# A PSUM bank reserved for the sums, another first transpose, and rounding steps tied to the gated rows, in a hash-attention and SwiGLU kernel

## The chip, the core and the metric

The kernel runs on one core of one Trainium2 chip. The metric is the device time of one execution in microseconds, median of three runs. An execution begins with its inputs in DRAM and ends when the output is in DRAM. The core has a matrix engine (PE, with its weight loads shown apart as PEld), a vector engine (DVE), a scalar engine (ACT), a general engine (POOL) and an engine that only issues transfers (SP). Each engine works through its own list of instructions; engines wait for each other through semaphores.

## The reference

Attention with a hash mask, and a gated feed-forward block on its result, all in 32-bit floats:

```python
# q, k, v: (4, 8, 768, 64); proj: (64, 6)
q_bits = einsum('bhsd,dk->bhsk', q, proj) > 0          # six sign bits for each row
k_bits = einsum('bhsd,dk->bhsk', k, proj) > 0
mask   = q_bucket[:, :, :, None] == k_bucket[:, :, None, :]
scores = where(mask, q @ k^T / 8, -1e9)
attn   = exp(scores - max);  attn = attn / (sum(attn) + 1e-9)
x      = attn @ v                                      # as (3072, 512) for what follows
g, val = x @ w_gate, x @ w_val                         # w: (512, 1536), 64-bit floats
out    = (g * sigmoid(g) * val) @ w_out                # w_out: (1536, 512)
```

The three weight matrices come in as 64-bit floats. The kernel reads them as pairs of 32-bit words and rounds them to 32-bit floats itself.

## The kernel before

**Rounds.** Work is cut into 32 rounds. A round is one batch, one pair of heads and one half of the 768 queries (`u` in the main loop L711 to L769 counts in steps of `NCH` = 6 key chunks; round number = `u / 6`). In each round TensorE computes six scores (`score`, L456: for both heads a 32-bit product of the transposed query and key, then a bf16 product of their sign bits, which pushes pairs of different buckets down), ACT takes the exponential of each score tile (L467) into a ring of six weight tiles, TensorE multiplies them by v (`attend`, L476), DVE adds the six weight tiles up (`add`, L487 and L491), TensorE sums that over the partitions with a matrix of ones (`norm`, L501, tile `sum`), and DVE takes its reciprocal (L504) and scales the product with v (L506, L507). Only then is the half of `xT` done that the feed-forward block reads.

**Front of a pair of heads.** `front` (L380) makes the transposed q and k and their sign bits. For the first pairs it transposes on TensorE (`tps`, L388; ACT copies out, L391) and hashes with `hash_bits` (`hps`, L405; ACT takes signs, L398; DVE scales those of k, L400). From the sixth pair on DVE transposes (L431), and `hash_blocks` (L411 to L415) does all four hash products into one PSUM tile.

**PSUM.** There are eight banks. `av` has one. All others are one pool of seven, `banks` (L66): the two score tiles of each chunk, `tps`, `hps`, `sum`, the six accumulators of an up-projection (`up`) and the three of a down-projection (`po`). A tile waits until the last reader of the tile that had its bank before is done.

**Feed-forward.** From round 8 (`LATE`, L450) each round also runs a list of `atoms`: single products of Strassen schemes. `both` (L554) is one up-projection of 14 atoms of size 1: seven products for the gate and seven for the value, in turn, with ACT copies (L591), DVE sums (L537), tanh on ACT (L519) and two DVE steps (L520, L524). Its last two products, in the two `a` accumulators, are read by L520 and L524 at the end of the list. `down_strassen` (L612) has seven atoms of size 2 per chunk. Weights of the up-projection come back from a DRAM scratch `ram` by POOL's transfers (`bring`, L322) into two `places`.

**Rounding the weights.** `prepare` (L345) is a generator of single DVE steps. For each of 36 pieces of 128 x 512 weights, `narrow` (L294) has three: L303, L305 and L308. Before them ACT makes two passes over the piece (`scale_to`, L286 and L287), which need the piece's 512 KB of words. `load_words` (L251) has POOL fetch the words, a few pieces ahead, into the buffers that a finished piece leaves. After eight pieces of a block, `form` (L324) adds four sums per pair (L337) and writes them to `ram`. The main loop advances this generator by hand: `prepare_on(2)` and `prepare_on(6)` in each round ahead of `norm` (L737, L739), and in the atom loop 0.7 steps for each unit of size (L759 to L761). `scale_ahead` (L290) puts the ACT passes of the next two or three pieces into ACT's list; it is called before `attend` and after every atom. The first piece also carries a test of how the words round: L282, L283, L285, L300 and L310 (through `bits_a` and `bits_b`).

**Order.** `manual_schedule` is on: instructions stand in each engine's list in the order of the program text, and none is moved. So the place of a call in the main loop decides what an engine does first. In the gating rounds `chores` puts the steps of the next pair's front behind single atoms: for the hash products after the second atom.

Of the kernel before, what the change touches and what calls it, by code (L numbers as in the profile page):

```python
# [8 lines left out]
FP32 = mybir.dt.float32  # L9
BF16 = mybir.dt.bfloat16  # L10
I32 = mybir.dt.int32
U16 = mybir.dt.uint16
ALU = mybir.AluOpType
# [5 lines left out]
def kernel(  # L19
# [11 lines left out]
    nc = tc.nc  # L31
# [3 lines left out]
    P = 128  # L35
# [27 lines left out]
    wraw = ctx.enter_context(tc.tile_pool(name="wraw", bufs=2))  # L63
    dram = ctx.enter_context(tc.tile_pool(name="dram", bufs=1, space=bass.MemoryType.DRAM))
    av_ps = ctx.enter_context(tc.tile_pool(name="av_ps", bufs=1, space=PSUM))
    banks = ctx.enter_context(tc.tile_pool(name="ps", bufs=7, space=PSUM))  # L66

    ctx.enter_context(tc.manual_schedule())

    def bank(name):  # L70
        return banks.tile([P, 512], FP32, tag="ps", name=name)


    pairs = [(b, pr) for b in range(B) for pr in range(NP)]
# [176 lines left out]
    def load_words(done, queue=nc.gpsimd):  # L251
        for i in range(len(words), len(pieces)):
# [6 lines left out]
            else:  # L259
# [2 lines left out]

    progress = {"late": False, "piece": 0, "scaled": 0, "blocks": 0}

    bits_a, bits_b = (formed[x].rearrange("p n m -> p (n m)").bitcast(I32)[:, 0:PIECE]
                      for x in range(2))

    def scale_to(count):

        free = NJ * (progress["blocks"] + 2)
        if free >= 2 * NJ * DF // PIECE:
            free = len(pieces)
        for i in range(progress["scaled"], min(count, free, len(pieces))):
            t, w = words[i], pieces[i][0]
            top = t.rearrange("p f w -> p (f w)").bitcast(U16)
            top = top.rearrange("p (f w) -> p f w", w=4)[:, :, 1]
            if i == 0:


                nc.vector.tensor_single_scalar(bits_a, t[:, :, 0], 29, op=ALU.logical_shift_right)  # L282
                nc.vector.tensor_scalar(bits_b, t[:, :, 0], scalar1=28, scalar2=1,  # L283
                                        op0=ALU.logical_shift_right, op1=ALU.bitwise_and)
                nc.vector.tensor_tensor(bits_a, bits_a, bits_b, op=ALU.add)  # L285
            nc.scalar.activation(w, t[:, :, 1].bitcast(FP32), AF.Copy, scale=2.0**-112)  # L286
            nc.scalar.activation(t[:, :, 0], top, AF.Copy, scale=2.0**-13 * (1 + 2.0**-17))  # L287
            progress["scaled"] = i + 1
# [5 lines left out]
    def narrow(i):  # L294
        progress["piece"] = i
        t, w = words[i], pieces[i][0]
        lo, hi = t[:, :, 0], t[:, :, 1]
        wi = w.bitcast(I32)
        if i == 0:
            nc.vector.tensor_tensor(bits_b.bitcast(FP32), bits_a, lo, op=ALU.not_equal)  # L300
        scale_to(i + 1)

        nc.vector.tensor_single_scalar(wi, wi, 3, op=ALU.logical_shift_left)  # L303
        yield True
        nc.vector.scalar_tensor_tensor(out=wi, in0=hi, scalar=-(1 << 31), in1=wi,  # L305
                                       op0=ALU.bitwise_and, op1=ALU.bitwise_or)
        yield True
        nc.vector.tensor_tensor(wi, wi, lo, op=ALU.add)  # L308
        if i == 0:
            nc.vector.scalar_tensor_tensor(out=w, in0=bits_b.bitcast(FP32), scalar=1e4, in1=w,  # L310
                                           op0=ALU.mult, op1=ALU.add)
        progress["piece"] = i + 1
        load_words(i)
        yield True
# [50 lines left out]
    def prepare_on(n):  # L365
        for _ in range(n):
            next(preparing, None)
# [12 lines left out]
    def front(n):  # L380
# [27 lines left out]

        def hash_blocks():

            tile_ = bank("hps")  # L411
            for i, (name, half) in enumerate((name, half) for name in "kq" for half in range(2)):
                nc.tensor.matmul(tile_[i * BLOCK : (i + 1) * BLOCK, 0:HQ],  # L413
                                 hash_w[:, 0:BLOCK], T[name, n][:, half * HQ : (half + 1) * HQ],
                                 start=True, stop=True)  # L415

            def evict(name, half):
                i = 2 * (name == "q") + half
                ps = tile_[i * BLOCK : (i + 1) * BLOCK, 0:HQ]
                for to in (0, D):  # L420
                    scale = sign(name, half, slice(to, to + BLOCK), ps)
                    if scale:
                        more.append(scale)

            more = []
            return [lambda at=at: evict(*at) for at in
                    (("k", 0), ("k", 1), ("q", 0), ("q", 1))] + [lambda: [f() for f in more] and None]
# [9 lines left out]
        turns = [lambda x=x: transpose(*x) for x in order]  # L437
        hashes = [lambda x=x: hash_bits(*x) for x in order]
        if n == 0:
            return [turns[2], turns[0], turns[1], hashes[2], hashes[0], hashes[1], turns[3],  # L440
                    hashes[3]]
        return turns + hashes

# [49 lines left out]
    def norm(u):  # L493
        n, half, _ = units[u]
        b, pr = pairs[n]
        if half == 0:
            xT[b, pr] = xp.tile([P, S], FP32, tag="xT", name="xT")
        ps = bank("sum")
        t = acc.pop((n, half))
        for h in range(2):  # L500
            nc.tensor.matmul(ps[h * D : (h + 1) * D, 0:HQ], ones, t[:, h, :], start=True, stop=True)  # L501
        a = av.pop((n, half))
        r = att.tile([P, HQ], FP32, tag="r", name="r", bufs=1)
        nc.vector.reciprocal(r, ps[:, 0:HQ])  # L504
        e = att.tile([P, 1], FP32, tag="e", name="e")
        nc.vector.tensor_scalar(e, a[:, HQ : HQ + 1], scalar1=EPS, scalar2=None, op0=ALU.mult)  # L506
        nc.vector.scalar_tensor_tensor(out=xT[b, pr][:, half * HQ : (half + 1) * HQ],  # L507
                                       in0=a[:, 0:HQ], scalar=e, in1=r,
                                       op0=ALU.add, op1=ALU.mult)
        if pr == NP - 1 and half == 1:  # L510
            push_ffn(b)
# [187 lines left out]
    def prepare_pair(count):  # L699
        for _ in range(count):  # L700
            rest.extend(f for f in steps.pop(0)() or [] if f)
# [2 lines left out]
        while todo:  # L704
            todo.pop(0)()

    prepare_pair(5)
    finish(rest)
    N = len(units)
    credit = ahead = 0.0  # L710
    for u in range(0, N, NCH):  # L711
        n, half, _ = units[u]
        gating = u >= LATE
# [3 lines left out]
                nc.gpsimd.memset(t[:, :, HQ:AW], 1.0)  # L717
        for c in range(NCH):
            score(u + c)
            if u == 0 and c in (1, 2, 4):  # L720
                prepare_pair(1)
                finish(rest)
            if c:
                add(u + c)
# [21 lines left out]
        if n + 1 < len(pairs):  # L746
            if half == 0:
                steps = front(n + 1)
                chores = [None, steps.pop(0), None, steps.pop(0)]
            else:  # L750
                chores = [None, steps.pop(0)]

        credit += 14 if n < 2 * NP else 15.75
        end = True
        while atoms and (credit > 0 or not end):
            size, atom, end = atoms.pop(0)
            credit -= size
            atom()
            ahead += 0.7 * size  # L759
            prepare_on(int(ahead))  # L760
            ahead %= 1  # L761
            scale_ahead()
            for _ in range(size):
                if chores:
                    step = chores.pop(0)
                    chores.extend(step and step() or [])
# [37 lines left out]
```

The softmax here doesn't subtract the row's maximum and nothing guards it: scores larger than these inputs give would overflow.

## Time and profile before

Median 1028.34 us (1027.86 to 1030.48); the profiled execution spans 1028.6 us.

| stage | us | what PE does |
|---|---|---|
| start | 0 to 8 | nine idle products, transposes and hashes of the first pair |
| rounds 0 to 7 | 8 to 113 | attention alone, weights are rounded beside it |
| rounds 8 to 13 | 113 to 306 | attention and up-projections of batch 0, weights are rounded beside it |
| rounds 14 to 31 | 306 to 863 | attention and feed-forward |
| end | 863 to 1029 | six up-projections and the last down-projections |

A period, in what follows, is the time from the first `up` of a round to the first product of the next round's feed-forward. Where nothing holds PE up, the profile shows two lengths: 27.99 us (438.24 to 466.23) for a round without hash products, and 28.97 us (409.27 to 438.24) for one with them. A time with two figures such as "204.88 0.81" in a line of the trace is start and duration in microseconds; "[2.47 <-ACT room L467]" is the idle time before it and what ended it. In the lines the tile `room` is an area shared by weights, ring tiles and weight pieces, and `wo`, `hid` and `words` hold pieces too.

### The profile page before, as it was taken

How to read it: one execution, taken by the hardware profiler on the slowest of the kernel's cores; microseconds unless marked ns; L12 is line 12 of the kernel's file. 1: busy time of each engine (PE TensorE's matmuls, PEld its weight loads, DVE VectorE, ACT ScalarE, POOL GpSimd, SP SyncE). 2: the span in 40 equal slices, each digit the busy share in tenths (PEclk: the TensorE clock that was granted, in tenths of full speed). 3: DMA queues.
4: the chain of work that ended last, by engine and by line, in shares of the span. 5: the costliest groups of instructions: out<-in, count | busy, mean ns of one | idle time of the engine just before them, and what ended most of it. 6: DMA issues, size and time to landing. Idle time of an engine off the chain costs nothing.

```text
span 1028.6 us, 12425 instructions
## 1 busy us (share of the span) xinstructions
PE 1014.7 (99%) x4597; PEld 610.6 (59%) x4597; DVE 624.5 (61%) x1012; ACT 418.8 (41%) x905; POOL 99.3 (10%) x192
## 2 busy tenths in 40 slices
PE   9999999999999999999999999999999999999998
PEld 4444455555557775555556677555555787555687
DVE  5999987869895445565656472565656451525521
ACT  6776647365452413544352421534435201232200
POOL 2212022321100000000000000000000000101000
PEclk9999999999999999999999999999999999999999
DMA  7656485744622114242321203233222000333101
GB/s 212 196 163 201 120 216 203 212 162 156 172 72 52 37 31 107 72 103 82 84 81 37 62 21 93 59 82 95 72 72 72 21 21 31 109 97 113 31 26 36
DMA packets 113884, 99.90 MB, mean 97 GB/s; under 512 B 86976, under 2 KB 97216, under 8 KB 113824
## 3 DMA queue, kind: packets, MB, share of 16 engines
q0 software_dynamic: 19104, 73.28, 21.7%
q1 hardware_dynamic: 93920, 25.64, 11.3%
q8 instruction: 36, 0.59, 0.2%
q10 hardware_dynamic: 800, 0.20, 0.1%
q14 instruction: 24, 0.20, 0.1%
HBM read 81.79 MB, written 17.30 MB: 96 GB/s over the span
## 4 chain that ended last, share of the span: by engine, by line
PE 81%; DVE 10%; issue 4%; DMA 3%; ACT 2%; POOL 1%; DVEq 0%; POOLq 0%
PE up L533 36%; PE po L533 21%; PE sc L464 11%; PE av L476 9%; DVE acc L491 2%; DMA words<-in_moe_w_out_dram 2%; DVE r L504 2%; PE sum L501 1%; DVE room L305 1%; PE hps L413 1%; DVE room L337 1%; DVE room L308 1%; ACT A L467 1%; PE hps L405 1%; DVE room L303 1%
## 5 line engine op out<-in xcount | busy, mean ns | idle before, releaser
L533 PE MATMUL up<-xT,room 128*128 128x384 f32 x768 | 263.5, 489 | 0.0
L533 PEld LDWEIGHTS up<-xT,room 128*128 128x128 f32 x768 | 143.9, 190 | 109.7 <-issue 15.2
L533 PE MATMUL up<-xc,room 128*128 128x384 f32 x576 | 198.3, 487 | 2.0 <-ACT hid L591 1.5
L464 PE MATMUL sc<-qT,kT 64*128 64x384 f32 x768 | 164.3, 498 | 7.3 <-DVE e L506 3.3
L533 PEld LDWEIGHTS up<-xc,room 128*128 128x128 f32 x576 | 109.0, 190 | 79.8 <-ACT hid L591 2.8
L537 DVE TENSOR_TENSOR c<-c,up 128x384 f32<-128x384 f32 x72 | 39.8, 552 | 151.9 <-PE up L533 151.9
L491 DVE TENSOR_TENSOR acc<-acc,A 128x768 f32<-128x768 f32 x128 | 122.7, 958 | 14.6 <-ACT A L467 1.6
L322 POOL DMA_DIRECT2D room<-ram x96 | 52.0, 542 | 671.9 <-PE up L533 662.4
L467 ACT ACTIVATE A<-sc 128x384 f32<-128x384 f32 x256 | 105.9, 492 | 7.9 <-PE sc L464 7.8
L464 PEld LDWEIGHTS sc<-qT,kT 64*128 64x128 f32 x768 | 69.6, 188 | 62.9 <-issue 45.5
L661 ACT COPY o<-po 128x256 f32<-128x256 f32 x48 | 17.9, 372 | 199.2 <-PE po L533 199.1
L504 DVE RECIPROCAL r<-sum 128x384 f32<-128x384 f32 x32 | 81.7, 2554 | 27.1 <-PE sum L501 27.1
L476 PE MATMUL av<-A,vraw 128*64 128x386 f32 x512 | 88.4, 487 | 0.0
L519 ACT ACTIVATE th<-c 128x384 f32<-128x384 f32 x72 | 37.6, 522 | 104.4 <-DVE c L537 104.2
L537 DVE TENSOR_TENSOR o<-o,po 128x256 f32<-128x256 f32 x36 | 15.2, 421 | 102.2 <-PE po L533 61.1
L467 ACT ACTIVATE room<-sc 128x384 f32<-128x384 f32 x128 | 54.3, 488 | 38.6 <-PE sc L464 38.3
L533 PE MATMUL po<-wo,hid 128*128 128x256 f32 x288 | 66.9, 382 | 0.0
L464 PE MATMUL sc<-qb,kb 64*128 64x384 bf16 x384 | 66.7, 324 | 0.2 <-DVE kb L400 0.2
L533 PE MATMUL po<-wo,room 128*128 128x256 f32 x288 | 66.3, 380 | 0.0
L533 PE MATMUL po<-room,hid 128*128 128x256 f32 x288 | 66.1, 379 | 0.0
L476 PEld LDWEIGHTS av<-A,vraw 128*64 128x64 f32 x512 | 36.8, 137 | 46.2 <-issue 45.3
L591 ACT COPY c<-up 128x384 f32<-128x384 f32 x72 | 34.4, 478 | 70.9 <-PE up L533 70.7
(113 smaller groups left out, 1041.3 us busy)
## 6 DMA issues: line engine op xcount, KB each, us to landing
room<-ram POOLq DMA_DIRECT2D x48, 512.0 KB, 4.7
room<-ram POOLq DMA_DIRECT2D x48, 384.0 KB, 3.9
vraw<-in_v_dram SPq DMA_DIRECT2D x16, 384.0 KB, 3.2
ram<-room POOLq DMA_DIRECT2D x12, 512.0 KB, 4.1
out_dram<-o SPq DMA_DIRECT2D x48, 128.0 KB, 1.7
qraw<-in_q_dram SPq DMA_DIRECT2D x48, 96.0 KB, 3.2
kraw<-in_k_dram SPq DMA_DIRECT2D x46, 96.0 KB, 3.4
words<-in_moe_w_out_dram POOLq DMA_DIRECT2D x8, 512.0 KB, 4.7
```

The costliest lines, as they stand in the source:

```text
L303: nc.vector.tensor_single_scalar(wi, wi, 3, op=ALU.logical_shift_left)
L322: nc.gpsimd.dma_start(places[k % 2][:, PARTS[go], :], ram[k % NG][:, PARTS[go], :])
L464: nc.tensor.matmul(sc[h], x["k", n][rows, ks], x["q", n][rows, qs], start=start, stop=not start)
L467: nc.scalar.activation(weights(u)[:, h, 0:HQ], sc[h], AF.Exp, scale=SCALE)
L476: nc.tensor.matmul(ps[h * D : (h + 1) * D, 0:AW], raws["v", n][:, h, c, :], a[:, h, :], start=c == 0, stop=c == NCH - 1)
L491: nc.vector.tensor_tensor(acc[n, half], acc[n, half], a[:, :, 0:HQ], op=ALU.add)
L504: nc.vector.reciprocal(r, ps[:, 0:HQ])
L519: nc.scalar.activation(th, g, AF.Tanh, scale=0.5)
L533: nc.tensor.matmul(ps, a, x, start=start and i == 0, stop=i == len(pairs_) - 1, skip_group_check=True)
L537: nc.vector.tensor_tensor(o, a, b, op=op)
L591: nc.scalar.copy(tile_of(g, spot), c)
L661: nc.scalar.copy(o, c)
```

## The change

Four edits. A pool of one bank, `sm_ps`, holds `sum` and the hash tile of `hash_blocks`; the shared pool shrinks from seven banks to six. The first pair's front transposes k before q, and does the second half of k after the first score and not before it; hash products in gating rounds move from the second atom to the fifth. The test on the first weight piece goes. In the atom loop, rounding steps go one per unit of size for the first ten units of a round's list (and then none), and ACT's passes are put ahead only from the sixth unit on. The aim is that sums no longer hold up the banks that scores need, and that the end of a round's gated rows is free of rounding work.

```diff
-    banks = ctx.enter_context(tc.tile_pool(name="ps", bufs=7, space=PSUM))
+    sm_ps = ctx.enter_context(tc.tile_pool(name="sm_ps", bufs=1, space=PSUM))
+    banks = ctx.enter_context(tc.tile_pool(name="ps", bufs=6, space=PSUM))
...
+    def odd_bank(name):
+        return sm_ps.tile([P, 512], FP32, tag="sm", name=name)
...
-    bits_a, bits_b = (formed[x].rearrange("p n m -> p (n m)").bitcast(I32)[:, 0:PIECE]
-                      for x in range(2))
...
-            if i == 0:
-                nc.vector.tensor_single_scalar(bits_a, t[:, :, 0], 29, op=ALU.logical_shift_right)
-                nc.vector.tensor_scalar(bits_b, t[:, :, 0], scalar1=28, scalar2=1,
-                                        op0=ALU.logical_shift_right, op1=ALU.bitwise_and)
-                nc.vector.tensor_tensor(bits_a, bits_a, bits_b, op=ALU.add)
...
-        if i == 0:
-            nc.vector.tensor_tensor(bits_b.bitcast(FP32), bits_a, lo, op=ALU.not_equal)
...
-        if i == 0:
-            nc.vector.scalar_tensor_tensor(out=w, in0=bits_b.bitcast(FP32), scalar=1e4, in1=w,
-                                           op0=ALU.mult, op1=ALU.add)
...
         def hash_blocks():
-            tile_ = bank("hps")
+            tile_ = odd_bank("hps")
...
         if n == 0:
-            return [turns[2], turns[0], turns[1], hashes[2], hashes[0], hashes[1], turns[3],
+            return [turns[0], turns[2], hashes[0], hashes[2], turns[1], hashes[1], turns[3],
                     hashes[3]]
...
-        ps = bank("sum")
+        ps = odd_bank("sum")
...
-    prepare_pair(5)
+    prepare_pair(4)
...
-            if u == 0 and c in (1, 2, 4):
+            if u == 0 and c in (0, 1, 2, 4):
                 prepare_pair(1)
...
-                chores = [None, steps.pop(0)]
+                chores = [None, None, None, None, steps.pop(0)]
...
+        part = 0
         while atoms and (credit > 0 or not end):
             size, atom, end = atoms.pop(0)
             credit -= size
             atom()
-            ahead += 0.7 * size
-            prepare_on(int(ahead))
-            ahead %= 1
-            scale_ahead()
+            part += size
+            if part < 11:
+                prepare_on(size)
+            if part > 5:
+                scale_ahead()
```

More of the change, by code (lines that the diff above doesn't have):

```diff
@@ L705, in finish @@
             todo.pop(0)()
-    prepare_pair(5)
+    prepare_pair(4)
     finish(rest)
     N = len(units)
-    credit = ahead = 0.0
+    credit = 0.0
     for u in range(0, N, NCH):
```

## The prediction

> **What bounds the kernel now.** I read the page's busy times and slices first, then stretches of the span, then who waited for whom, and last the order of time round each wait of PE.
>
> ```profile
> PE 1014.7 (99%) x4597; PEld 610.6 (59%) x4597; DVE 624.5 (61%) x1012; ACT 418.8 (41%) x905; POOL 99.3 (10%) x192
> DVE  5999987869895445565656472565656451525521
> PEclk9999999999999999999999999999999999999999
> ```
>
> PE is busy 99%, so 13.9 us of idle time are all that shows. But ends of matmuls are modelled, so I measure PE by the start of one product to the start of the next. DVE's row says where PE is not alone: nines in the first quarter, five or six later.
>
> ```profile
> 22.00:41.00 19.00, 17.14 (x100) 7.59 (x96) 18.09 (x27) 14.38 (x33) 3.75 (x6) 1.00 0.61 183
> 104.00:116.00 12.00, 12.00 (x68) 5.36 (x70) 11.38 (x17) 8.36 (x18) 1.13 (x2) 1.00 0.72 196
> 180.00:220.00 40.00, 37.53 (x160) 20.12 (x158) 32.59 (x54) 15.96 (x35) 11.13 (x18) 0.96 0.66 185
> 552.00:862.00 310.00, 310.00 (x1448) 200.03 (x1447) 166.63 (x262) 104.59 (x233) 12.92 (x24) 1.00 0.20 57
> ```
>
> (Columns: window, length, busy PE, PEld, DVE, ACT, POOL, granted clock, DMA share, GB/s.) In rounds 0 to 7 DVE is full: its rows in order of time carry no idle time from 17.22 to 138.26 us. From 180 to 220 PE has 2.47 us of idle time and a clock of 0.96. After 552 PE never stops; nothing can be won there.
>
> ```profile
> PE sc L464 <- DVE e L506: 3.3, 5, 1.6
> PE sc L464 <- ACT room L467: 2.5, 1, 2.5
> PE sc L464 <- DVE c L520: 1.4, 2, 1.2
> ```
>
> Three kinds of wait. The first is the edit's target: a fifth score gets the bank of the last `sum` and waits for its reciprocal (L504, just ahead of L506). In order of time, DVE, PE and ACT:
>
> ```profile
> 22.21 0.69 DVE L310 SCALAR_TENSOR_TENSOR room<-room 128x512 f32<-128x512 f32 x1
> 25.77 2.55 DVE L504 RECIPROCAL r<-sum 128x384 f32<-128x384 f32 x1
> 28.38 0.92 PE L464 MATMUL sc<-qT,kT 64*128 64x384 f32 x4 [1.56 <-DVE e L506]
> 208.15 1.01 PE L464 MATMUL sc<-qT,kT 64*128 64x384 f32 x1 [2.47 <-ACT room L467]
> 206.52 0.66 ACT L286 ACTIVATE wo<-words 128x512 f32<-128x512 f32 x1 [4.87 <-DMA words<-in_moe_w_out_dram]
> ```
>
> The last two are one wait: ACT stood 4.87 us for a piece's words, the exponentials behind it came late, and scores found no bank.
>
> Lost time by start of one period to the next (`up` at 123.18, 153.33, 184.09, 216.87, 245.83, 276.77, 306.05) against 27.99 and 28.97 us undisturbed: rounds 8 to 13 lose 2.16, 1.79, 4.79, 0, 2.95, 0.31, **12.0 us in sum**. Rounds 1 to 7, first score to first score (22.51 to 113.45 = 90.94 us), against 4 x 12.96 and 3 x 11.61 (those lengths less their waits): 4.3 us lost.
>
> **What the Trainium skill says.** "Perfetto Trace Analysis", Optimization Strategy: a gap that repeats on the engine that should be full can mean that PSUM ran out for the next tile. The trace agrees: five waits, 3.3 us. "TensorE: Matmul & The Clock Gate", Architectural detail: ACT and DVE work strictly first in, first out. It agrees: exponentials at 207.63 stood behind that L286. The same page, What's actually happening: about 3.4 us of an idle PE halve its clock until it has been busy as long. Here 2.47 us were followed by products of 1.01 us where others take 0.48 to 0.59, and 40 us at 0.96 are 1.6 us lost: part of round 10's 4.79. "DMA: Bandwidth & Descriptors", Anatomy of one DMA: 2.0 us and bytes/436e3, an estimated 3.2 us for 512 KB. The page shows 4.7 for `words`; one issued at 197.10 landed at 206.5, 9.4 us. The measurements decide.
>
> **The change, part by part.**
>
> *Test removed.* L282, L283, L285, L300, L310: 0.42 + 0.42 + 0.69 + 0.69 + 0.69 = 2.9 us of DVE, at 18 to 23 us, with DVE full behind it. The reciprocal at 25.77 moves to about 23.1 (it needs `sum`, done at 22.5). ACT's wait of 1.12 us for L283 goes as well, hidden.
>
> *Own bank for sums, rounds 0 to 7.* PE's waits for L506 go: up to 4.3 us. But DVE is full, so PE gains nothing beyond DVE: `sum` needs the last add, which stands behind last round's reciprocal. I went through the rounds with PE lengths above and DVE's own (reciprocals at 25.77, 38.46, 50.44, 64.17, 75.62, 88.87, 101.22, 113.64; 2.6 us earlier each). PE runs ahead until it waits for adds in round 8: last add at 121.99 - 2.6 = 119.4, `sum` 0.75 later, first `up` at 120.3, not 123.18. **-2.9 us.**
>
> *Six banks in turn.* Steady rounds: ACT starts exponentials 1.1 us after a score; the fourth score (2.5 us in) now needs both tiles of the first, read 2.0 us in. No cost. After an `up`, scores now get banks c, b, a in pairs: both `a` banks at 18.06 + 1.7 = 19.8 us after the first `up`, where before the last was needed at 20.6. In steady rounds L524 frees it at 19.9 (486.06 - 466.16) less the 0.78 of hashes, 19.1: hidden. While pieces are rounded DVE is later; that is in the sum below. From one `up` list to the next at the end, the pool gives the banks freed first: old c becomes a. No cost.
>
> *First key first.* k's sign is done while q's still runs, so DVE's 0.32 us (8.77) hides: first scores about 0.3 us earlier; the second half's transposes (0.35) follow. Nothing of it survives DVE's bound.
>
> *Hash products after the fifth atom, in the odd bank.* They wait for that round's reciprocal. Queued behind them: all of PE. First `up` + 6.45 us, against the end of reciprocals at +2.6 steady, 4 to 5.5 in rounds 8 to 13: hidden. L400 (1.33 us) now stands between late L520s; worked through for 466 us, L524 ends 0.1 later. Hidden.
>
> *Rounding steps.* Per round 8 + 10 where there were 8 + 9.8, but bunched: a piece per three atoms (3.9 us), not per 5.5. After a piece DVE's L308 frees its buffer, POOL issues the next words 0.55 us later (131.87 to 132.42), they land 4.5 us later (between 3.75, at 127.62, and 9.4). ACT's passes (1.3 us) wait there, now ahead of tanh and not ahead of exponentials. So the cost moves: tanh late, L520 and L524 late, `a` banks late. Round 10, from first `up`: L507 ends 4.1; L305 and L308 to 5.5; words issued 6.0, land 10.5; passes and tanh to 12.3; second piece done 9.3, words 9.8 to 14.3, passes and tanh to 16.1; L520 16.6, then L337, two L537 and L524, and the last two pairs, 0.47 each: last L524 20.4. Needed 19.8: 0.6 lost, 1.3 with words of 5.2 us (186.34 to 191.54): 1.0, where it was 4.79 (no exponential waits for words, no slow clock). In the same way round 8 loses 2.6 (its third passes wait for words issued after L507), 9: 2.3, 11: 2.0 (four pieces in one list and the hashes' eight signs on ACT), 12: 2.7 (1.0 to 4.4: one load goes behind a `bring` of 512 KB, as at 258.45, 8.0 us), 13: 0.3. Sum 10.9 for 12.0: **-1.1 us.**
>
> *Sum:* 1028.34 - 2.9 - 1.1 = **1024.3 us**.
>
> **Rivals.**
> A (forecast): first stage 2.9, second about even: 1021.5 to 1025.9.
> B: words land before ACT asks, and rounds 8 to 13 lose 1 us each in five periods: 5 for 12.0, 1028.34 - 2.9 - 7 = 1018.4. For it: edits put words ahead of `bring` in POOL's list. Against: words took over 4 us in all but two waits.
> C: waits change places. Loads 0.7 us slower in rounds 8 to 10, late ends of 11 and 12 (2.7, 4.4): 15.4 for 12.0, so +3.4 - 2.9: 1028.8. For it: DVE and ACT both carry the same work in the same period.
> D, slower: two rounds get a 9.4 us load ahead of tanh. DVE stands in order behind it, 4.9 us each, and one stop reaches the slow clock, 1.7 us: 1024.3 + 11.5 = 1035.8. For it: such loads occur, and tanh now stands behind them. Against: only 197.10 and 258.45 were so late.
>
> **How the numbers follow.** A 0.42, B 0.22, C 0.22, D 0.14. 0.3% is 3.1 us: faster is below 1025.2, slower above 1031.4. Nine tenths of A and all of B are faster: 0.60; C and the rest of A the same: 0.26; D slower: 0.14. Range 1017 to 1032: B's better end and D's worse are left out.
>
> **What would show it.** Right: no L464 waits for L506; reciprocals of rounds 1 to 7 about 2.6 us earlier; first `up` near 120.3; clock 1.00 from 180 to 220; after 300 us the same lengths, 27.99 and 28.97. Wrong: PE waiting for L501's input before round 8; scores waiting for L520 or L524 in rounds 9 to 13 for over 3 us each; `hps` (L413) waiting for a reciprocal; any new wait after 320 us, where I cost everything at nothing.

## The result, and the profile after

The changed kernel takes 1033.66 us (median of 4 runs, 1032.34 to 1034.75) where the kernel before took 1028.10 in the same comparison (4 runs, 1027.55 to 1030.48). The ratio is 1.0049, 95% interval [1.0028, 1.0070]: about 5 us slower. The forecast was 1024.3, its range ended at 1032.0.

On the page of the changed kernel, the busy times and two rows of the slices:

```profile
PE 1020.4 (99%) x4597; PEld 616.2 (60%) x4597; DVE 622.8 (60%) x1007; ACT 419.9 (41%) x905; POOL 99.5 (10%) x192
DVE  5999987879785445565656472465656450524521
PEclk9999999999999999999999999999999999999999
```

PE is "busy" 5.7 us longer than before with the same 4597 products: waits shorter than the modelled ends, and products at half clock, count as busy. So starts of products have to be compared again. The same stretches as in the prediction:

```profile
22.00:41.00 19.00, 19.00 (x118) 9.30 (x118) 17.62 (x24) 15.04 (x35) 4.14 (x7) 1.00 0.63 190
180.00:220.00 40.00, 39.55 (x163) 20.84 (x159) 33.68 (x57) 17.84 (x38) 9.96 (x17) 1.00 0.68 189
552.00:862.00 310.00, 310.00 (x1447) 199.15 (x1444) 166.04 (x261) 105.26 (x233) 12.97 (x24) 1.00 0.20 57
```

In the first stretch PE issues 118 products where it issued 100 before, without a gap; from 180 to 220 the clock is full. Both are as forecast. Now PE's waits:

```profile
PE sc L453 <- DVE c L509: 3.8, 4, 2.5
PE sum L490 <- DVE acc L480: 2.2, 2, 2.0
```

(Line numbers moved: L453 is the score, L509 and L513 are the two gate steps that were L520 and L524, L526 the sums that were L537, L490 the product `sum`.) The waits for the reciprocal's reader and for exponentials are gone. Scores now wait for gates for 3.8 us where it was 1.4, and a new kind has come: one `sum` waits 2.0 us for the last add.

By starts of periods, the first `up` comes at 120.33 (forecast 120.3; before 123.18). From there:

| period | 8 | 9 | 10 | 11 | 12 | 13 | sum | 21, 29 |
|---|---|---|---|---|---|---|---|---|
| lost before, us | 2.16 | 1.79 | 4.79 | 0 | 2.95 | 0.24 | 11.9 | 0, 0 |
| forecast | 2.6 | 2.3 | 1.0 | 2.0 | 2.7 | 0.3 | 10.9 | 0, 0 |
| lost after | 2.74 | 1.98 | 2.47 | 2.35 | 5.34 | 0.86 | 15.7 | 0.87, 0.87 |

(The prediction has 0.31 for period 13 before. Its start of round 14, 306.05, comes from a view that puts starts 0.07 later than the view of the other starts; with one view it is 305.98, and the sum 11.9.) All other periods are as long as before (27.99, 28.97, 28.06, 29.04, 46.12). So 2.85 us are won ahead of 120 us, 3.8 lost in rounds 8 to 13, and 1.7 in rounds 21 and 29: 2.7 us slower, as the two profiled spans are (1028.57 and 1031.27). The medians are 5.6 us apart; the profiled execution of before, 1030.65 us, was one of its slower ones.

The 0.87 of round 21 in order of time, the changed kernel (its first `up` is at 524.09; the first line, L389, is the scaling of k's hash signs):

```profile
539.21 1.31 DVE L389 TENSOR_SCALAR kb<-kb,columns 32x384 bf16<-32x384 bf16 x4
543.02 0.55 DVE L526 TENSOR_TENSOR room<-hid 128x384 f32<-128x384 f32 x1
543.61 0.56 DVE L526 TENSOR_TENSOR room<-room,hid 128x384 f32<-128x384 f32 x1
544.09 0.55 DVE L526 TENSOR_TENSOR hid<-hid 128x384 f32<-128x384 f32 x1
544.55 0.55 DVE L509 SCALAR_TENSOR_TENSOR c<-c,up 128x384 f32<-128x384 f32 x1
545.16 1.25 PE L453 MATMUL sc<-qT,kT 64*128 64x384 f32 x3
545.21 0.55 DVE L513 SCALAR_TENSOR_TENSOR hid<-c,up 128x384 f32<-128x384 f32 x1
545.90 0.32 PE L453 MATMUL sc<-qb,kb 64*128 64x384 bf16 x1
```

The kernel before at the same place (first `up` at 523.12):

```profile
542.48 0.55 DVE L537 TENSOR_TENSOR hid<-hid 128x384 f32<-128x384 f32 x1
542.95 0.55 DVE L520 SCALAR_TENSOR_TENSOR c<-c,up 128x384 f32<-128x384 f32 x1
543.60 0.56 DVE L524 SCALAR_TENSOR_TENSOR hid<-c,up 128x384 f32<-128x384 f32 x1
544.08 0.81 PE L464 MATMUL sc<-qT,kT 64*128 64x384 f32 x4
544.88 0.81 PE L464 MATMUL sc<-qT,kT 64*128 64x384 f32 x4
```

Three sums for the first down-projection (`early` in `push_ffn`) stand on DVE between the batch's last pair of gates and the one ahead of it. In both kernels the last gate ends after the third score could start. Before, the bank that it frees was wanted by the fourth score (544.88, 0.72 us later). After, the third score is cut in two: its first tile is begun at 545.16, as L509 has ended (544.55 + 0.55), its second at 545.81, as L513 has (545.21 + 0.55).

### The profile page after: what moved, and what is told of

Read it like the earlier page. It is cut to its first block, busy times and chain, and to the rows that moved or that the text cites. A ratio compares the mean times of both kernels' runs of the same rounds, so it can differ in the third digit from the quotient of the medians.

```text
span 1031.3 us, 12454 instructions
## 1 busy us (share of the span) xinstructions
PE 1020.4 (99%) x4597; PEld 616.2 (60%) x4597; DVE 622.8 (60%) x1007; ACT 419.9 (41%) x905; POOL 99.5 (10%) x192
## 4 chain that ended last, share of the span: by engine, by line
PE 83%; DVE 8%; issue 4%; DMA 3%; ACT 2%; POOL 0%; DVEq 0%; POOLq 0%
PE up L522 34%; PE po L522 21%; PE sc L453 14%; PE av L465 10%; DVE acc L480 2%; PE sum L490 2%; PE hps L394 1%; DMA words<-in_moe_w_out_dram 1%; DVE r L493 1%; DVE c L509 1%; DMA room<-in_moe_w_out_dram 1%; PE hps L402 1%; PE tps L377 1%; DVE room L326 1%; DVE room L297 1%
## 5 line engine op out<-in xcount | busy, mean ns | idle before, releaser
L453 PE MATMUL sc<-qT,kT 64*128 64x384 f32 x768 | 169.4, 499 | 4.0 <-DVE c L509 3.8
L526 DVE TENSOR_TENSOR c<-c,up 128x384 f32<-128x384 f32 x72 | 39.8, 553 | 146.9 <-PE up L522 146.6
L453 PEld LDWEIGHTS sc<-qT,kT 64*128 64x128 f32 x768 | 73.7, 188 | 60.6 <-issue 43.3
L526 DVE TENSOR_TENSOR o<-o,po 128x256 f32<-128x256 f32 x36 | 15.2, 422 | 104.4 <-PE po L522 63.4
L453 PE MATMUL sc<-qb,kb 64*128 64x384 bf16 x384 | 71.1, 325 | 0.0
```

The lines of the kernel that those rows point to most:

```text
L453: nc.tensor.matmul(sc[h], x["k", n][rows, ks], x["q", n][rows, qs], start=start, stop=not start)
L526: nc.vector.tensor_tensor(o, a, b, op=op)
```

## The experiments

Ratios are to the kernel before in the same session, whose median varied from 1029.2 to 1031.8 between sessions; so kernels are compared by their ratios. "Theory 1" was that the bunched rounding steps cost, "theory 2" that one bank less in the rotation does.

**The parts, one at a time.** First, the rounding steps: the changed kernel with the old placing, and the kernel before with the new.

```diff
-            part += size
-            if part < 11:
-                prepare_on(size)
-            if part > 5:
-                scale_ahead()
+            ahead += 0.7 * size
+            prepare_on(int(ahead))
+            ahead %= 1
+            scale_ahead()
```

> The changed kernel with the rounding steps of the atom loop as before (0.7 steps for each unit of size, ACT passes put ahead after every atom); bank, test and first key stay changed. Theory 1 (the bunched rounding steps put ACT's waits for words ahead of tanh and so hold the a banks in rounds 8 to 13): the second stage loses what it did before, the first keeps its 2.9 us, and only the three waits of 0.87 us in rounds 13, 21 and 29 stay: about 1028 us. Theory 2 (with six banks the scores want both a banks 0.8 us earlier, in every round in which DVE is late): little comes back, 1031 to 1033 us, and rounds 8, 10 and 12 still show scores that wait for L509 or L513.

> The kernel before with only the new distribution of rounding steps. Theory 1: 5 to 6 us slower than before, 1033 to 1034 us, with round 12 losing about 5 us as in the changed kernel. Theory 2: within 1.5 us of before, since seven banks leave the last a bank until the fourth score.

Measured: undone 1034.39 us, 1.0046 [1.0029, 1.0063], no different from the whole change; alone 1029.27 us, 0.9986 [0.9977, 0.9995], a gain of 1.4 us. Theory 1 falls.

The bank of its own with six in turn, and the hash products behind the fifth atom, on the kernel before:

```diff
-    banks = ... bufs=7
+    sm_ps = ... bufs=1        # sum, hash tile
+    banks = ... bufs=6
-                chores = [None, steps.pop(0)]
+                chores = [None, None, None, None, steps.pop(0)]
```

> The kernel before with only the bank of its own for sums and hash tile, six in turn, and the hash products after the fifth atom. Theory 1: no waits for the reciprocal in rounds 1 to 7, but DVE is full there, so at most 1 us is won; 2.6 us lost in rounds 13, 21 and 29: about 1030 us. Theory 2: rounds 8 to 13 lose up to 0.8 us each as well: 1032 to 1034 us.

Measured: 1035.56 us, 1.0062 [1.0040, 1.0084]. First `up` at 122.81, where it was 123.18: the bank wins 0.4 us in the first stage. Rounds 21 and 29 took 0.86 us more, rounds 8 to 13 lost 14.6. So this part alone costs about as much as the whole change (1.0049; the intervals overlap). The waits for the reciprocal's reader that it takes away come back as waits for adds:

```profile
PE sum L505 <- DVE acc L495: 4.3, 4, 2.0
```

The test removed, and the first key first, each alone on the kernel before:

> The kernel before without the test of the first words and nothing else. Theory 1 (DVE is full up to round 8, so what it is spared there comes off the end): 2.9 us of DVE less, the reciprocal of round 0 some 2.6 us earlier, first gate product near 120.6, and 2.0 to 2.9 us off the end: 1025.5, ratio 0.997 to 0.998. Rival (rounds 8 to 13 take it back, since the same loads of words and the same 2.5 us waits come whatever the start): first gate product early, first down-projection where it was, ratio 0.999 to 1.000.

> The kernel before with the first key ahead of the first query and nothing else. Theory (DVE sets rounds 0 to 7): first score 0.3 us earlier, first gate product where it was within 0.2 us, no change in the time: ratio 0.9992 to 1.0005. Rival: the 0.3 us, or the half microsecond by which the changed kernel's first score came earlier, goes through to the end: ratio 0.9995 or less.

Measured: without the test 1028.95 us, 0.9981 [0.9968, 0.9994], first `up` at 120.61, and the first down-projection 2.4 us earlier than before; its theory holds. First key alone: 1030.50 us, 1.0007 [0.9998, 1.0016], first score at 7.70 instead of 8.05 and first `up` at 123.16 instead of 123.18: no effect at the end, as DVE sets that stage. (In the 15 profiles with this order the first score comes at 7.41 to 8.31, on average at 7.7; in the five with the old one at 7.91 to 8.14, on average at 8.0.)

**All but the bank.** The changed kernel with seven banks in one rotation again. (Its expectation puts the hash products behind the first atom; as before, it is the second.)

```diff
-    sm_ps = ... bufs=1
-    banks = ... bufs=6
+    banks = ... bufs=7
-            tile_ = odd_bank("hps")
+            tile_ = bank("hps")
-        ps = odd_bank("sum")
+        ps = bank("sum")
```

> The changed kernel with seven banks in one rotation again, for sums and hash products too, and the hash products after the first atom: the test is gone, the first key comes first, the rounding steps are in their new places. Theory 2 (one bank less is what costs): rounds 13, 21 and 29 back at 28.97 us, scores in rounds 8 to 13 wait for the last gate bank at most 2 us in all, time = before - 1.4 (the rounding steps alone, as measured) - 2.5 (the test): 1024 to 1026, ratio 0.995 to 0.9975; the changed kernel is then 8 to 9 us slower than it for its banks. Rival (parts of the change hinder one another: without the bank of its own, sums wait again and eat up what the test frees): five waits of a score for the reciprocal's reader, 3 us, ratio 0.998 to 1.000.

Measured: 1026.48 us, 0.9954 [0.9937, 0.9971]. This beats both kernels. Between it and the changed kernel lie 0.95% in ratio, 7.2 us in medians and 6.2 us between the profiled spans: that is what the bank edit costs, together with the later hash products that go with it. Its waits:

```profile
PE sc L450 <- DVE c L506: 2.9, 2, 2.3
PE sc L450 <- DVE e L492: 1.5, 3, 0.6
PE up L519 <- DVE c L523: 1.4, 2, 0.8
```

(L506 is the gate step, L492 the reciprocal's reader.) The wait that the bank was to remove is still there, 1.5 us in three pieces, yet its first `up` is at 120.74, 0.4 us behind the changed kernel's: PE had that time to spare. Periods 8 to 13 lose 1.62, 1.52, 1.99, 0.91, 4.84 and 0 us; rounds 21 and 29 nothing. Against the changed kernel's spans: 0.4 won in the first stage, 4.9 lost in rounds 8 to 13, 1.7 in 21 and 29.

**The sums at a batch's end.** They were put behind the last atom, with six banks and with seven:

```diff
-        atoms[at] = (size, lambda: (early(), last()), end)
+        atoms[at] = (size, lambda: (last(), early()), end)
```

> The changed kernel with the three sums of hidden rows for the first down-projection (the three L526 steps ahead of the last L509 of a batch) put behind the last atom of the up list and not ahead of it. If these three steps are what holds the a banks in rounds 13, 21 and 29, their periods fall from 29.84 to 28.97 us and the time by 2.6 us, to about 1031 us. If it is L389 (four steps of k's signs, now late in the list), nothing changes.

> As the run with seven banks, with the three sums that the first down-projection needs put behind the last atom of the batch. Theory 2: with seven banks the last gate bank is needed half a score later, 0.84 us, so the three sums of 0.56 us hid already, and nothing is won: within 0.05% of the run with seven banks, rounds 13, 21 and 29 at 28.97 in both. Rival (the sums cost by themselves): 2.6 us less than the run with seven banks.

Measured with six: 1031.71 us, 1.0012 [1.0003, 1.0020], rounds 13, 21 and 29 at 28.97 again. With seven: 1026.43 us, 0.9954 [0.9937, 0.9971], the same as without the move. So with six banks the place of the three sums costs 2.6 us (3 x 0.87), and with seven nothing. The 0.87 isn't theirs alone, though: it takes the later hash products too, as is shown below.

**Six banks for everything.** One bank of the kernel before lies unused (`bufs=6`).

> The kernel before with six banks in one rotation instead of seven (one bank lies unused), sums and hash products still among them, their place in the order as before. Theory 2 (scores behind a list of gate products find one bank less): rounds 21 and 29 take 0.87 us more, rounds 8 to 13 lose 4 to 8 us more than the 12 of before, and rounds 0 to 7 wait longer for the reciprocal's reader: ratio 1.006 to 1.012, at or above the 1.0062 of the bank of its own. Rival (it was the bank of its own, one tile for sums and hash products which must wait for each other, and the later hash products, that cost): ratio 1.000 to 1.003, below the 1.0062.

Measured: 1049.35 us, 1.0176 [1.0155, 1.0197], worse than either theory had it. The top line of its waits says why:

```profile
PE up L533 <- ACT qb L398: 10.5, 7, 1.5
```

The hash tile keeps its bank until ACT has taken eight signs, and with six in the rotation the next `up` wants it; of the later odd rounds with an up-projection none is spared (rounds 17, 19, 21, 25, 27 and 29 take 1.8 to 2.0 us more). So given six, a bank of its own for the hash tile and the sums, with the hash products behind the fifth atom, is far better than sharing with them behind the second. What costs would then be the seventh bank, which is missing from the rotation and idle but for sums and hash products; the next runs try that.

**The earlier need by itself.** In the kernel with seven banks, a small spare product takes one bank. Ahead of the first score, first:

```diff
+        if u > LATE:
+            ps = bank("spare")
+            nc.tensor.matmul(ps[0:D, 0:8], ones, ident[:, 0:8], ...)
         for c in range(NCH):
             score(u + c)
```

> The run with seven banks, with a spare product of eight columns ahead of the scores of rounds 9 to 31, in a bank of the rotation: it takes the bank that the sum left, so that the third score wants the last gate bank and not the fourth, as with six. Sums, hash products (after the second atom) and clock are as with seven banks. Theory 2 (a score that finds its bank 0.84 us too early a need is the cost): rounds 13, 21 and 29 take 0.87 us more, rounds 9 to 12 lose 1.5 to 3 us more in sum; beside 0.1 us a round for the product itself (seen in steady rounds) 3.5 to 6 us more than the run with seven banks, ratio 0.999 to 1.003. Rival (the cost came from what went with it, the hash products, the long wait, the clock): only the product's own 2 us, ratio 0.996 to 0.998.

Measured: 1030.26 us, 1.0000 [0.9990, 1.0010]; every period from round 13 on takes 0.21 us more, rounds 21 and 29 too, and rounds 8 to 12 take 0.2 us less in sum. The 18 periods make 3.8 us, which is the distance to seven banks in medians. This run missed its aim: the spare product waits for no gate, so the two gate banks were wanted no earlier. So the product stands between the second and third score in the next:

```diff
+        held = u // NCH in (9, 10, 11, 12, 13, 14, 22, 30)
+        if held:
+            spare_bank = bank("spare")
         for c in range(NCH):
             score(u + c)
+            if held and c == 1:
+                nc.tensor.matmul(spare_bank[0:D, 0:8], ones, ident[:, 0:8], ...)
```

> The run with seven banks, with a spare product of eight columns between the second and the third score of rounds 9 to 14, 22 and 30: it takes one bank there, so that both gate banks are wanted by the third score, as with six; all else is as with seven banks (in the run before this one the spare product stood ahead of the first score, its bank came back ahead of the gate banks, and those were wanted no earlier; so that run shows only what the product costs, 0.21 us). Theory 2 (it is this need, half a score earlier, that costs): the periods of rounds 13, 21 and 29 take 0.8 to 1.1 us more than with seven banks, rounds 8 to 12 lose 1 to 3 us more in sum; 5 to 7 us more than seven banks with 1.7 for the products: ratio 1.0000 to 1.0025. Rival (the cost is that of the hash products and waits that go with a bank of its own): 0.21 us in each of eight rounds, 1.7 us, ratio 0.9965 to 0.9975.

Measured: 1031.62 us, 1.0002 [0.9992, 1.0012], 0.48% above seven banks: some 4.9 us, of which 8 x 0.21 = 1.7 are the products themselves. Periods 8 to 13 take 0.78, 0.66, 0.27, 0.65, 0.59 and 0.41 us more than with seven banks, 21 and 29 0.41. Less 0.21 each, that is 2.1 us in rounds 8 to 13 and 0.4 in the two others. In round 21:

```profile
543.16 0.55 DVE L510 SCALAR_TENSOR_TENSOR hid<-c,up 128x384 f32<-128x384 f32 x1
543.74 0.28 PE L710 MATMUL spare<-ident,ones 128*64 128x8 f32 x2
543.95 0.92 PE L450 MATMUL sc<-qT,kT 64*128 64x384 f32 x4
```

The gate ends at 543.71, and PE goes on at 543.74; by the trace it is the spare product that waits for the gate's bank, and the third score stands behind it. The product itself delays that score by 0.21, so the wait costs 0.20 and not 0.87, less than the 0.6 to 0.9 expected. But with the earlier need as the only change, each of the eight periods got longer by more than the product. Theory 2 holds in kind: the rival's ratio, at most 0.9975, lies outside the interval. Its size holds for this place of the hash products, behind the second atom, where the last gate of round 21 ends 21.03 us after the first `up` and not 21.67.

**With gates on time.** DVE's three rounding steps are left out from round 8 on, with seven banks and with the changed kernel's.

```diff
+        if not progress["bare"]:          # set when u == LATE
             nc.vector.tensor_single_scalar(wi, wi, 3, ...)
```

(The same ahead of the two other steps of `narrow`.)

> The run with seven banks, with DVE's three rounding steps left out of every piece rounded from round 8 on (the words are still loaded and scaled on ACT, the weights are then not exact): some 12 us less for DVE in each of rounds 8 to 12. Only its distance to the same kernel with the changed kernel's banks is asked. Both theories: rounds 8 to 12 lose less than the 10.9 us of the run with seven banks, since gates come on time; what is left is ACT's waits for words. Total 1016 to 1024, ratio 0.986 to 0.994.

> The changed kernel (a bank of its own, six in turn), with the same rounding steps left out from round 8 on. Theory 2 (six banks cost where DVE is late, because both gate banks are needed by the third score and not the fourth): DVE isn't late any more in rounds 8 to 12, so they lose the same as with seven banks within 1 us in sum, and only the three sums ahead of the last gate product remain, 0.87 us in each of rounds 13, 21 and 29: 1.5 to 3 us slower than the seven banks with the same left out. Rival (six banks cost in rounds 8 to 12 whatever DVE does, by scores, exponentials or up products that find no bank): the same 7 us slower as with the rounding steps in.

Measured: seven banks 1019.09 us, 0.9897 [0.9883, 0.9912]; the changed kernel's 1023.72 us, 0.9942 [0.9928, 0.9956]. The distance is 4.6 us (5.5 between the profiled spans): neither theory's 1.5 to 3, nor 7. Rounds 9, 10 and 12 now lose no more with six banks than with seven (1.3, 0, 1.6 for 1.5, 0, 1.6), as theory 2 says. What is left sits elsewhere: 0.86 us in each of rounds 21 and 29 and 1.2 in 13 (the batch's last lists, with the three sums); 1.4 in round 11; and 1.7 in round 8, which lost nothing with seven.

Round 11: with seven banks the last gate step L509 starts at 226.68, 0.42 us behind the first score; with six, its counterpart L512 starts 1.78 us behind the first score, and the third score waits for it:

```profile
225.63 1.31 DVE L392 TENSOR_SCALAR kb<-kb,columns 32x384 bf16<-32x384 bf16 x4
227.65 0.92 PE L456 MATMUL sc<-qT,kT 64*128 64x384 f32 x4
229.43 0.55 DVE L512 SCALAR_TENSOR_TENSOR c<-c,up 128x384 f32<-128x384 f32 x1
230.04 1.25 PE L456 MATMUL sc<-qT,kT 64*128 64x384 f32 x3 [0.46 <-DVE c L512]
```

The first line is the scaling of the hash signs, between gates, where the later hash products put it. Round 8 is the clock. In the changed kernel, PE and a stretch of the span:

```profile
119.54 0.87 PE L490 MATMUL sum<-acc,ones 128*64 128x384 f32 x4 [1.97 <-DVE acc L480]
```

```profile
120.58:123.99 3.41, 3.41 (x6) 1.71 (x6) 3.38 (x8) 0.48 (x1) 0.00 (x0) 0.50 0.00 0
```

With its own bank for the sums and without the test, PE runs ahead, so that its small waits of the first stage come together in one of 2.0 us. For 3.41 us, from 0.25 us after the first `up`, the granted clock is then 0.50: six products where the next such stretch has twelve, 1.7 us.

**Taking these away.** Hash products back behind the second atom:

> The changed kernel with the hash products of the odd rounds back after the first atom, in the bank that they share with the sums. Theory: they then wait for the reciprocal that reads the sum, which ends 2.6 us after the first gate product in steady rounds where the first atom ends at 1.3: PE stands for 1.3 us in each of rounds 17, 19, 25, 27 and 21, 29 and up to 3 us in rounds 9, 11, 13: 10 to 17 us slower than the changed kernel, ratio 1.014 to 1.021. Rival (the place of the hash products is part of what the bank edit costs, since their signs then stand between late gates): faster than the changed kernel, ratio 1.000 to 1.004.

Measured: 1036.58 us, 1.0065 [1.0048, 1.0083]. The expectation counted with the first atom; it is the second, 2.78 us behind the first `up` (469.17 to 471.95), and steady rounds don't wait at all. Rounds 9, 11 and 13 do:

```profile
PE hps L402 <- DVE e L495: 5.1, 3, 2.4
```

And rounds 21 and 29 take 29.20 us, not 29.84: of their 0.87 only 0.23 is left, though the three sums stand where they stood. In round 21 of this run, whose first `up` is at 526.13:

```profile
545.96 0.55 DVE L509 SCALAR_TENSOR_TENSOR c<-c,up 128x384 f32<-128x384 f32 x1
546.61 0.55 DVE L513 SCALAR_TENSOR_TENSOR hid<-c,up 128x384 f32<-128x384 f32 x1
```

The last gate ends 21.03 us after the first `up`, as in the kernel before (21.04), and 0.64 us earlier than in the changed kernel (21.67). So two things together make the 0.87: the three sums, and the scaling of the hash signs (L389), which the later hash products put among the last gates. Here the expectation's rival is right for these two rounds, while the waits for the reciprocal in rounds 9, 11 and 13 cost more than that.

Hash products after the third atom, then spare products against the long wait, then these two with the sums behind:

```diff
-                chores = [None, None, None, None, steps.pop(0)]
+                chores = [None, None, steps.pop(0)]
```

```diff
+        if u + 1 == LATE:
+            for _ in range(5):
+                nc.tensor.matmul(ps[0:D, 0:HQ], ones, xT[pairs[n - 1]][:, 0:HQ], ...)
```

> The changed kernel with the hash products of the odd rounds after the third atom and not the fifth. Theory 4 (behind the fifth atom their signs on ACT and their scaling on DVE stand between the late gates: 1.4 us in round 11 even without rounding steps): round 11 loses 1 to 1.5 us less, round 13 up to 0.5 us less, against waits for round 9's reciprocal of up to 1.1 us (2.4 us behind the second atom): ratio 1.0035 to 1.0045. Rival (the wait for the reciprocal is as long as what the gates win, as behind the second atom, 1.0065): ratio 1.0045 to 1.0060.

> The changed kernel with five spare products (1.9 us of PE, into the bank of the sums, overwritten by the sum) where PE stands for 2.0 us ahead of round 7's sum. Theory 3 (with a bank of their own for the sums PE runs ahead, its small waits come together in that one, and the clock halves for 3.41 us right behind it, as at 120.58): no half clock near 121 us, first gate product still at 120.3 to 120.6, round 8 loses 1.0 to 1.2 us where it was 2.7, 1.2 to 1.7 us off the end: ratio 1.0030 to 1.0038. Rival (DVE is the bound there, and late gates of round 8 take back what the clock gives): full clock, but round 8 loses 2.5 us and more and the ratio stays at 1.0045 to 1.0053.

> The changed kernel with the spare products, the hash products after the third atom, and the three sums of the first down-projection behind the last atom. If the three causes are what the bank costs, and add up: 1033.7 - 1.5 (clock) - 0.5 (hash products) - 2.6 (sums) = 1029, ratio 0.999 to 1.001; seven banks keep the rest, some 2.5 us, where gates are late in rounds 8 to 13. If something else costs, ratio 1.0025 or more.

Measured: hash products after the third atom 1033.43 us, 1.0035 [1.0022, 1.0049]. Round 11 lost 0.5 us less, rounds 21 and 29 took 29.20 us as behind the second atom, waits for the reciprocal came to 1.0 us; the interval holds both expectations, and the run doesn't decide. Spare products: 1033.71 us, 1.0034 [1.0021, 1.0046]. They went ahead of round 7's sum and took 3.2 us; the long wait was ahead of round 8's. It was used up all the same: no wait for adds, no half clock near 121, and the first `up` 0.9 us later, counted from the first score. But round 8 lost 2.46 us where it had lost 2.74. In the profile that is the rival: late gates took back what the clock gave. The ratio lies in the theory's range, and its interval reaches the rival's, so the time doesn't decide. All three: 1033.35 us, 1.0041 [1.0028, 1.0054], "something else costs". It is slower than the run with the sums alone behind the last atom (1.0012). In part that is the spare products: with 3.2 us they took more than PE had to spare, and the first `up` comes at 121.84 where it came at 120.51. Round 13 still loses 0.89, without the sums.

The same three with the late rounding steps left out (and three spare products, 1.9 us):

> The changed kernel with DVE's rounding steps left out from round 8 on, and with the spare products (three of them, 1.9 us), the hash products after the third atom, and the three sums behind the last atom. Theory: where gates aren't late, clock (1.7), sums (2.7) and hash products (1.4) are all that six banks and a bank of its own cost beside seven (4.6 us measured), so this comes to 1018.5 to 1020.5, ratio 0.989 to 0.991, like seven banks with the same left out (0.9897); with the steps in, the same three edits gave nothing since late gates set the end. Rival (there is a cost that none of the three names): ratio 0.9925 or more.

Measured: 1020.07 us, 0.9901 [0.9886, 0.9915], against 0.9897 with seven banks. The first `up` is at 120.82, the clock stays full in round 8, and rounds 13, 21 and 29 lose nothing. So where gates are on time, the sums, the hash products and the clock together are the cost of the bank edit as far as the measurement tells: 1.0 us of 4.6 is left in medians, and each ratio is known to about 0.0015. The share of the hash products is the least certain: round 11 still loses 0.97, and round 9 2.3 where it lost 1.3. With the rounding steps in, the same three edits together gave little. That a next late gate then holds the same score fits this, but no run shows it. Nor is there a run with seven banks and the hash products behind the fifth atom, so in rounds 8 to 13 the two parts of the bank edit are not wholly told apart.

## Why the prediction was wrong

**Right.** The test: 2.9 us of DVE gone, first `up` at 120.33 where 120.3 was forecast, and 0.9981 alone. The own bank in rounds 0 to 7: "PE gains nothing beyond DVE"; alone it moved 0.4 us. First key: nothing. The rounding steps: forecast -1.1, measured alone -1.4. The mechanism is the one given, but for the clock (below): passes on ACT wait for words ahead of tanh and no longer ahead of exponentials, as round 12 of the changed kernel shows:

```profile
263.35 0.66 ACT L280 ACTIVATE wo<-room 128x512 f32<-128x512 f32 x1 [2.88 <-DMA room<-in_moe_w_out_dram]
264.45 0.51 ACT L508 ACTIVATE th<-c 128x384 f32<-128x384 f32 x1
266.67 1.66 PE L453 MATMUL sc<-qT,kT 64*128 64x384 f32 x3 [2.48 <-DVE c L509]
```

Without the bank edit these terms come to 1026.48 us: the direction of the forecast, and its range, for three of the four edits.

**The step that failed** is "Six banks in turn". Its "No cost" rests on L524 freeing the bank "at 19.9 (486.06 - 466.16) less the 0.78 of hashes, 19.1: hidden", against a need at 19.8. That was read from round 19, and is right for it. It isn't for the last list of a batch: in round 21 the changed kernel's L513 ends at 545.21 + 0.55 - 524.09 = 21.7 us after the first `up`, and the need, 19.8 + 0.98 for a round with hash products, is 20.8. By the prediction's own arithmetic 0.9 us late; 0.87 was measured, and 0.86 in round 13. (Its 18.06 is the length of a list that follows another list; behind a `sum` it is 18.26, 438.24 to 456.50. The third score of round 21 would have started at 20.96, as before (544.08 - 523.12), so the gate is 0.7 late, and the score that is cut in two costs the rest.) Three L537 lines ahead of the last gates were in the trace, and only one kind of round was looked at.

A second term failed with it, under "Hash products": "L524 ends 0.1 later. Hidden." In round 19 the last gate ends 0.24 later than before (20.14 for 19.90), which is hidden; in round 21 0.63 later (21.67 for 21.04), and there it decides: with the hash products earlier, six banks cost that round 0.23. The prediction had named the sign itself: "any new wait after 320 us, where I cost everything at nothing".

**The sum for rounds 8 to 13**, into which late gates were put ("that is in the sum below"), was 10.9 us. Seven banks lose 10.9 in their profile, but by chance: 1.62, 1.52, 1.99, 0.91, 4.84 and 0, where 2.6, 2.3, 1.0, 2.0, 2.7 and 0.3 were forecast. The changed kernel loses 15.7. Round 10, the one walked through in full, was given 1.0; it lost 1.99 with seven banks and 2.47 with six. Of the 4.8 us missed, 0.86 are round 13; the rest is the earlier need, later hash signs and the clock. How these share it in the whole kernel stays open, since taking them away one by one, or all at once, did not give their sum.

**Hash products**, "hidden", held for rounds 17, 19, 25 and 27, and the wait for the reciprocal was hidden in all. In rounds 21 and 29 it did not hold, as said. In round 11 the signs land between late gates too: 1.4 us are lost there without the rounding steps, of which 0.46 came back with the products behind the third atom.

**The clock** was wrongly taken away for good. A full clock was right for 180 to 220 us. It came back twice, at 120.58 (behind the gathered wait that the prediction had itself: "PE runs ahead until it waits for adds in round 8") and at 267.35, behind the 2.48 us above. The second is part of round 12's 5.34 for 2.7, and isn't the banks': seven banks show it at 264.60 and lose 4.84.

**What is left.** The forecast is 9.3 us below the median. Between the profiles, 6.7 us of it are seen: 4.8 in rounds 8 to 13, 1.7 in rounds 21 and 29, and 0.2 in small differences. Most of the other 2.6 is a mix of two executions: the losses of before were read from a profiled execution of 1030.65 us, with 1.6 us of slow clock in it, and taken off a median of 1028.34.

Of the rivals, C ("waits change places") had the right kind, but took the loss from slower loads; D came near in time (1035.8), but for 9.4 us loads ahead of tanh: the longest wait of ACT in round 12 was 3.07 us.

## What to carry to other kernels

A bank reserved for a tile that lives for a few microseconds is a bank less for everything else; ask who takes it up in the rotation, and move each need forward accordingly, in every kind of round, the last of a batch too. A wait is worth removing only on the engine that sets the stage: here up to 4.3 us of PE's waits for the reciprocal's reader went and 0.4 came through; since DVE was full, PE waited for adds instead. When several late things may end at the same wait, taking one away can show nothing. It helped here to make the engine behind them idle first. And a wait can need two causes at once: the 0.87 went wholly with the sums moved, and for the most part with the hash products moved, so the two shares don't add up.

## What the hardware showed

Clock stretches come in multiples of 3.413 us. Those of the changed kernel are 116.05, 3.41, 143.36, 3.41 and 761.17 us long: 34, 1, 42, 1 and 223 times that. So I laid a grid of 3.413 us over each trace, from the start of its first full clock. Added up over one unit of the grid (gaps between products of over 0.15 us, by their modelled ends), PE's idle time was 1.9 us or more in 16 units of the kernels here, past the start, and the half clock followed at the end of each; of the units with less, 1.65, 1.43 and 1.25 us were followed by it too, while 1.80, 1.73 and four of 1.55 or 1.56 were not. So less than 3.41 us of idle time is enough, and it matters where it falls. The kernel with the bank edit alone had the same wait as the changed one:

```profile
122.01 0.87 PE L505 MATMUL sum<-acc,ones 128*64 128x384 f32 x4 [1.96 <-DVE acc L495]
```

but a unit of the grid ended in its middle, at 121.06, 1.01 us on one side and 0.95 on the other, and its clock stayed full.

So whether a half-clock stretch comes can differ between executions of one kernel. In 152 executions of the kernel before, taken beside the experiments, the mean granted clock was 1.0 in 71, with a median of 1029.06 us; 0.998, as in the profiled one with its one stretch of 3.41 us, in 58, with 1031.29; and 0.997 in 19, with 1033.14. One such stretch goes with some 2 us, as much as several of the edits here.
